# Retention chunks feeding a tanh-shrink MLP: one 64x64 excursion per chunk, single pairs of banks, earlier weight conversions

## The chip, the cores and the metric

The kernel runs on one core of a Trainium2 chip. The metric is device time in microseconds (us) of one execution. Profiled executions give a span, from the first to the last instruction, which is about 2 us shorter than the device time of the same execution.

## The reference

```python
# q, k, v: (4, 8, 768, 64); w_in: (512, 2048); w_out: (2048, 512)
gamma = 1.0 - 2.0 ** (-5.0 - np.arange(H, dtype=np.float32))
for t in range(S):                                   # retention, one state per batch and head
    state = gamma[None, :, None, None] * state + einsum('bhd,bhe->bhde', k[:, :, t], v[:, :, t])
    y[:, :, t] = einsum('bhd,bhde->bhe', q[:, :, t], state) / np.sqrt(D)
x = y.transpose(0, 2, 1, 3).reshape(B * S, H * D)    # 3072 tokens x 512
h = x @ w_in
out = (h - np.tanh(h)) @ w_out
```

The recurrence is computed in chunks of 128 tokens, 24 chunks in all. A **chunk** goes through four stages on TensorE: *turn* (8 transposes of k and q), *products* (k by v and k by q, 64 small matmuls), *outputs* (y from the state and half of the part inside the chunk) and *outputs_rest* (the other half). A **step** of the MLP is one tile: *up_step* (h, 16 matmuls), *shrink_step* (h - tanh h by ScalarE and VectorE, ends in g) and *downs* (o, 8 matmuls, two steps later). There are 96 steps. Weights arrive as 8-byte numbers and are *converted* by ScalarE, then VectorE, then GpSimd (POOL).

## The kernel before

All PSUM tiles of a chunk come from one function with two pairs of banks in rotation. Transposes, products and y of any chunk take the pair that is free next (only the transposes of chunks 0 to 3 use banks of o and h instead).

```python
def banks(name):
    return ps.tile([P, 2, BANK], F32, tag="t", name=name)      # the pool has bufs=2
```

The stages of a chunk, cut to the tiles and the copies that read them:

```python
def turn(ci, tag="t"):
    turned[ci] = [banks(f"kqTp_{ci}")]                # PSUM
    ...                                               # 8 transposes, whole array
def turn_copy(ci):
    nc.scalar.copy(out=t[:, ds(at, n)], in_=tp...)    # kqT, ScalarE, PSUM to SBUF
def products(ci):
    sp = banks(f"s_{ci}")
    ...                                               # 32 + 32 matmuls on 64x64 quarters
    nc.vector.tensor_tensor(m, halves[:, :, 0], ...)  # the mask
    ...                                               # two additions: states
def outputs(ci):
    yT = banks(f"y_{ci}")
    ...                                               # 32 of state, 16 of intra, on quarters
    def rest():
        intra(False)                                  # 16 more on quarters
        nc.scalar.copy(out=xT[n]..., in_=y)           # xT, ScalarE
```

The start is written out by hand, statement by statement. The loop over steps then places a chunk beside chosen steps:

```python
when = [4, 5, 6] + list(range(7, 28, 2)) + [28, 29, 30, 31]
with_chunk = {s: 6 + i for i, s in enumerate(when)}
for s in range(BEGUN, len(steps)):
    ci = with_chunk.get(s)
    if ci is not None:
        scale_chunk(ci + 2)
        outputs(ci)                    # first excursion to quarters
    ...
    up_step(s)
    if ci is not None:
        outputs_rest(ci)               # second excursion
        products(ci + 1)
        load_chunk(ci + 3)
    shrink_step(s)
    downs(LAG)
    if ci is not None:
        turn(ci + 2)
        turn_copy(ci + 2)
```

## Time and profile before

| | before |
|---|---|
| device time, median of 3 executions | 788.15 us (786.81 to 788.59) |
| span of the profiled execution | 786.7 us |
| end of the transposes of chunk 7, the last statement of the start | 82.25 us |
| rest, from there to the end | 704.45 us |
| TensorE idle in the start / in the rest | 22.9 us / 4.9 us |

The columns are the stretch, its length, the busy time and number of instructions of each engine, the granted clock, and the transfers:

```profile
0.00:82.25 82.25, 59.36 (x960) 43.21 (x960) 50.80 (x85) 35.50 (x68) 28.92 (x28) 0.83 0.72 165
82.25:786.70 704.45, 699.55 (x4545) 468.64 (x4544) 471.36 (x724) 334.75 (x593) 94.81 (x79) 1.00 0.16 42
```

Length minus busy time of TensorE is its idle time: 82.25 - 59.36 = 22.9 and 704.45 - 699.55 = 4.9. The start and the rest are thus two different programs, one bound by waits and one by TensorE, and everything below is told for each by itself.

### The profile page before, as it was taken

Reading aid. Unit: us, or ns where it says so; the run is one execution under the profiler, and the core shown is the slowest. Engines: PE = TensorE matmul, PEld = TensorE weight load, DVE = VectorE, ACT = ScalarE, POOL = GpSimd, SP = SyncE. Lnnn points to the kernel's source line nnn. Section 1 sums busy time; section 2 is a strip of 40 time slices with the busy share of each in tenths; the row PEclk is TensorE's granted clock in tenths of the full one; section 3 lists DMA queues with packets and bytes.
Section 4 is the critical chain, followed back from the end, with each engine's and each line's share of the span. In section 5 each row is a group of like instructions: output and inputs, shape, how many; then the busy total and the mean of one; then the engine's idle time right before and its main releaser. Section 6 shows DMA issues by size and latency. Waiting matters only on the chain.

```text
span 786.7 us, 13754 instructions
## 1 busy us (share of the span) xinstructions
PE 758.9 (96%) x5504; PEld 511.9 (65%) x5504; DVE 522.2 (66%) x808; ACT 370.2 (47%) x661; POOL 123.7 (16%) x106
## 2 busy tenths in 40 slices
PE   4869999999999999999999999999999999999997
PEld 4645776677667667666666666666666666666664
DVE  4676698789888875575666565566565656655654
ACT  3453566665655654443344444344444433444432
POOL 1155354333544441000000000000000000000000
PEclk9778999999999999999999999999999999999999
DMA  9953364443433422010000000000000000000000
GB/s 203 260 123 68 87 159 118 123 110 95 120 97 95 105 45 68 29 54 1 1 27 1 0 27 1 1 27 0 13 14 1 27 1 0 27 0 1 28 0 27
DMA packets 85711, 42.97 MB, mean 55 GB/s; under 512 B 76304, under 2 KB 76432, under 8 KB 85648
## 3 DMA queue, kind: packets, MB, share of 16 engines
q1 hardware_dynamic: 85504, 41.95, 21.2%
q8 instruction: 43, 0.70, 0.4%
q10 hardware_dynamic: 144, 0.15, 0.1%
q14 instruction: 20, 0.16, 0.1%
HBM read 35.80 MB, written 6.29 MB: 54 GB/s over the span
## 4 chain that ended last, share of the span: by engine, by line
PE 92%; DVE 4%; SPq 1%; issue 1%; ACT 1%; POOL 1%; DMA 1%; DVEq 0%; POOLq 0%; ACTq 0%
PE o L385 42%; PE h L353 42%; PE y L297 3%; PE kqTp L223 2%; PE s L257 1%; PE s L251 1%; SPq L199 1%; DVE head L176 1%; DVE head L174 1%; DMA raw<-in_moe_w_in_dram 1%; DVE a L261 0%; DVE power L178 0%; POOL low L179 0%; POOL w L183 0%; DVE head L172 0%
## 5 line engine op out<-in xcount | busy, mean ns | idle before, releaser
L385 PE MATMUL o<-w,g 128*128 128x512 f32 x768 | 351.8, 601 | 5.8 <-POOL w L183 5.3
L353 PE MATMUL h<-xT,w 128*128 128x256 f32 x1536 | 354.1, 384 | 3.0 <-POOL w L183 2.2
L353 PEld LDWEIGHTS h<-xT,w 128*128 128x128 f32 x1536 | 292.4, 192 | 71.8 <-issue 31.3
L385 PEld LDWEIGHTS o<-w,g 128*128 128x128 f32 x768 | 145.4, 192 | 152.6 <-issue 138.2
L362 ACT ACTIVATE u<-h 128x512 f32<-128x512 f32 x96 | 57.4, 598 | 268.6 <-PE h L353 268.6
L367 DVE TENSOR_TENSOR th<-h,th 128x512 f32<-128x512 f32 x96 | 66.2, 690 | 159.2 <-ACT th L363 159.2
L377 DVE COPY_PREDICATED g<-large,th 128x512 f32<-128x512 int32 x96 | 73.8, 769 | 10.6 <-DVE g L376 0.9
L370 DVE SCALAR_TENSOR_TENSOR h<-q,h 128x512 f32<-128x512 f32 x96 | 66.9, 697 | 10.4 <-DVE h L368 0.5
L372 DVE SCALAR_TENSOR_TENSOR h<-q,h 128x512 f32<-128x512 f32 x96 | 66.8, 696 | 10.0
L364 ACT ACTIVATE q<-u,tab 128x512 f32<-128x512 f32 x96 | 69.5, 724 | 0.0
L365 ACT ACTIVATE q<-u,tab 128x512 f32<-128x512 f32 x96 | 69.0, 719 | 0.0
L366 ACT ACTIVATE large<-u,tab 128x512 f32<-128x512 f32 x96 | 68.8, 716 | 0.0
L376 DVE TENSOR_TENSOR g<-h,u 128x512 f32<-128x512 f32 x96 | 66.3, 691 | 3.3
L368 DVE SCALAR_TENSOR_TENSOR h<-u,h 128x512 f32<-128x512 f32 x96 | 65.8, 685 | 0.0
L179 POOL TENSOR_TENSOR low<-low,power 128x512 f32<-128x512 f32 x31 | 39.6, 1277 | 157.4 <-DVE power L178 153.7
L363 ACT ACTIVATE th<-h 128x512 f32<-128x512 f32 x96 | 57.1, 594 | 0.0
L233 ACT COPY kqT<-kqTp 128x1024 f32<-128x1024 f32 (+1 forms) x28 | 24.8, 891 | 53.2 <-PE kqTp L223 53.0
L261 DVE TENSOR_TENSOR a<-s,tab 128x512 f32<-128x512 f32 x24 | 16.6, 690 | 41.5 <-PE s L257 41.4
L183 POOL TENSOR_TENSOR w<-low,head 128x512 f32<-128x512 f32 x31 | 39.8, 1283 | 2.4
L331 ACT COPY xT<-y 128x512 f32<-128x512 f32 x24 | 14.1, 587 | 53.5 <-PE y L297 53.5
L208 POOL TENSOR_TENSOR q<-q,tab 128x512 f32<-128x512 f32 x20 | 22.3, 1115 | 14.9 <-DMA q<-in_q_dram 14.9
L297 PEld LDWEIGHTS y<-kqT,state 64*64 64x64 f32 x704 | 12.9, 134 | 17.9 <-issue 11.7
(37 smaller groups left out, 372.2 us busy)
## 6 DMA issues: line engine op xcount, KB each, us to landing
k<-in_k_dram SPq DMA_DIRECT2D x24, 256.0 KB, 4.6
q<-in_q_dram SPq DMA_DIRECT2D x24, 256.0 KB, 5.1
v<-in_v_dram SPq DMA_DIRECT2D x24, 256.0 KB, 5.4
raw<-in_moe_w_out_dram SPq DMA_DIRECT2D x12, 512.0 KB, 3.7
out_dram<-sum SPq DMA_DIRECT2D x24, 256.0 KB, 2.0
raw<-in_moe_w_in_dram SPq DMA_DIRECT2D x14, 256.0 KB, 3.0
raw<-in_moe_w_in_dram SPq DMA_DIRECT2D x28, 128.0 KB, 4.2
raws<-in_moe_w_out_dram SPq DMA_DIRECT2D x4, 512.0 KB, 5.4
```

The source lines that it names most:

```text
L353: nc.tensor.matmul(hp[:, ts(i, TH)], w1[:, c, ts(2 * m2 + i, P)], xT[n // 2][:, c, ts(n % 2, TH)], start=(i == 0 and c == 0), stop=(c == N ...
L362: nc.scalar.activation(u, hp, AF.Square)
L364: nc.scalar.activation(q0, u, AF.Square, bias=bias0)
L365: nc.scalar.activation(q1, u, AF.Square, bias=bias1, scale=math.sqrt(A))
L366: nc.scalar.activation(large, u, AF.Relu, bias=bias_m)
L367: nc.vector.tensor_tensor(th, hp, th, op=ALU.subtract)
L368: nc.vector.scalar_tensor_tensor(hp, in0=u, scalar=R, in1=hp, op0=ALU.subtract, op1=ALU.mult, reverse0=True)
L370: nc.vector.scalar_tensor_tensor(hp, in0=q0, scalar=C0, in1=hp, op0=ALU.add, op1=ALU.mult)
L372: nc.vector.scalar_tensor_tensor(hp, in0=q1, scalar=A * C1, in1=hp, op0=ALU.add, op1=ALU.mult)
L376: nc.vector.tensor_tensor(flat, hp, u, op=ALU.mult)
L377: nc.vector.copy_predicated(flat, large.bitcast(I32), th)
L385: nc.tensor.matmul(o_p[j], gT[n, m2][:, i, ts(j, P)], w2[:, 2 * m2 + i], start=(first and i == 0), stop=(last and i == 1))
```

## The change

The intent has three parts. **One excursion**: the quarter work of three chunks (rest of one, products of the second next, outputs of the next) is put together between downs and the next up_step, so that TensorE leaves whole-array work once for each chunk instead of twice. **Banks**: as this work overlaps two chunks' y, y of even and odd chunks share one fixed pair, and transposes and products share the other, each with one buffer. **Conversions first**: in the start, the weight conversions stand ahead of the masks and shrinks in the queues of VectorE and POOL.

```diff
-    def banks(name):
-        return ps.tile([P, 2, BANK], F32, tag="t", name=name)
+    def banks(tag, name):
+        return ps.tile([P, 2, BANK], F32, tag=tag, name=name, bufs=1)
... (k and q get two buffers instead of three, v four)
-            turned[ci] = [banks(f"kqTp_{ci}")]
+            turned[ci] = [banks("t", f"kqTp_{ci}")]
...
-        sp = banks(f"s_{ci}")
+        sp = banks("t", f"s_{ci}")
...
+    y_banks = banks("y", "y").rearrange("p r (two n t) -> p two r n t", two=2, n=2)
...
-        yT = banks(f"y_{ci}")
-        y = yT[:, :, : 2 * P].rearrange("p r (n t) -> p r n t", n=2)
+        y = y_banks[:, ci % 2]
... (the "seen" copies: four small ones instead of two)
... (the start; here from chunk 2 on, cut)
+    convert(2)
     products(2)
...
-    convert(2)
+    convert(3)
     outputs(2)
     products(3)
...
-    convert(3)
+    convert(4)
     outputs(3)
+    convert(5)
     outputs_rest(3)
...
+    up_step(1)
     shrink_step(0)
-    up_step(1)
-    convert(4)
-    shrink_step(1)
     scale_chunk(4)
-    convert(5)
     up_step(2)
     turn(4)
     turn_copy(4)
-    shrink_step(2)
+    shrink_step(1)
+    convert(6)
     downs(LAG)
     products(4)
     scale_chunk(5)
-    convert(6)
     turn(5)
     turn_copy(5)
     convert(7)
-    up_step(3)
+    shrink_step(2)
     outputs(4)
     products(5)
... (the loop)
-    when = [4, 5, 6] + list(range(7, 28, 2)) + [28, 29, 30, 31]
-    with_chunk = {s: 6 + i for i, s in enumerate(when)}
+    when = [4, 5, 6] + list(range(7, 28, 2)) + [28, 29, 30, 31, 32]
+    with_chunk = {s: 5 + i for i, s in enumerate(when)}
...
-            scale_chunk(ci + 2)
-            outputs(ci)
+            scale_chunk(ci + 3)
+            outputs_rest(ci)
+            products(ci + 2)
+            load_chunk(ci + 4)
+            if ci + 1 < NCH:
+                outputs(ci + 1)
         up_step(s)
-        if ci is not None:
-            outputs_rest(ci)
-            products(ci + 1)
-            load_chunk(ci + 3)
         shrink_step(s)
         downs(LAG)
         if ci is not None:
-            turn(ci + 2)
-            turn_copy(ci + 2)
+            turn(ci + 3)
+            turn_copy(ci + 3)
```

More of the change, by code (lines that the diff above doesn't have):

```diff
@@ L197, in load_chunk @@
         for nm, src in (("k", k), ("q", q), ("v", v)):
-            t = inp.tile([P, H, D], F32, tag=nm, name=f"{nm}_{ci}")
+            t = inp.tile([P, H, D], F32, tag=nm, name=f"{nm}_{ci}", bufs=4 if nm == "v" else 2)
             nc.sync.dma_start(out=t, in_=src[b, :, ts(j, P), :].rearrange("h p d -> p h d"))
@@ L281, in outputs @@
         j = ci % CPB
-        n, nj = divmod(ci, BLK)
-        if nj == 0:
-            xT[n] = xp.tile([P, NP, BLK * P], F32, tag="xT", name=f"xT_{n}")
-        vh = loaded.pop(ci)[2]
+        vh = loaded[ci][2]
         qT = turned.pop(ci)[:, 1]
         a_, st = masked.pop(ci), states.pop(ci)
-        yT = banks(f"y_{ci}")
-        y = yT[:, :, : 2 * P].rearrange("p r (n t) -> p r n t", n=2)
+        y = y_banks[:, ci % 2]
         begun = set()
@@ L318, in outputs @@
         intra(True)
-        flat = yT.rearrange("p r w -> p (r w)")
         for col in range(2):
-            r = ds(D * col, D)
-            s0, s1 = 2 * P - 1 - D, BANK + 2 * P - 1
-            if col:
-                s0, s1 = 2 * P - 1, BANK + 2 * P - 1 - D
-            nc.scalar.copy(out=seen[r], in_=flat[r, s0 : s1 + 1 : s1 - s0])
+            for r in range(2):
+                nc.scalar.copy(out=seen[ds(D * col, D), r : r + 1],
+                               in_=y[ds(D * col, D), r, 1, ds(D * ((r + col) % 2), 1)])
         def rest():
+            n, nj = divmod(ci, BLK)
+            if nj == 0:
+                xT[n] = xp.tile([P, NP, BLK * P], F32, tag="xT", name=f"xT_{n}")
             intra(False)
+            loaded.pop(ci)
             nc.scalar.copy(
@@ L437 @@
     load_weights(1)
-    load_chunk(2)
     scale_chunk(0, nc.vector)
@@ L443 @@
     products(0)
+    load_chunk(2)
     turn(1, "h")
@@ L455 @@
     outputs_rest(1)
-    load_chunk(4)
-    load_weights(6)
-    load_weights(7)
     up_step(0)
@@ L463 @@
     scale_chunk(3, nc.vector)
+    convert(2)
     products(2)
+    load_chunk(4)
+    load_weights(6)
+    load_weights(7)
     turn(3, "o")
     turn_copy(3)
-    convert(2)
+    convert(3)
     outputs(2)
     products(3)
+    load_chunk(5)
     outputs_rest(2)
-    load_chunk(5)
-    convert(3)
+    load_weights(8)
+    convert(4)
     outputs(3)
+    convert(5)
     outputs_rest(3)
-    load_weights(8)
-    load_chunk(6)
+    up_step(1)
     shrink_step(0)
-    up_step(1)
-    convert(4)
-    shrink_step(1)
     scale_chunk(4)
-    convert(5)
     up_step(2)
@@ L485 @@
     turn_copy(4)
-    shrink_step(2)
+    shrink_step(1)
+    convert(6)
+    load_weights(9)
     downs(LAG)
     products(4)
+    load_chunk(6)
     scale_chunk(5)
-    convert(6)
-    load_weights(9)
     turn(5)
@@ L495 @@
     load_weights(10)
-    up_step(3)
+    shrink_step(2)
     outputs(4)
     products(5)
-    outputs_rest(4)
     load_chunk(7)
-    shrink_step(3)
-    outputs(5)
+    up_step(3)
     scale_chunk(6)
-    downs(LAG)
-    outputs_rest(5)
-    load_chunk(8)
     turn(6)
     turn_copy(6)
+    outputs_rest(4)
     products(6)
+    load_chunk(8)
+    outputs(5)
+    shrink_step(3)
+    downs(LAG)
     scale_chunk(7)
```

## The prediction

> **What bounds the kernel now.** I read the page's busy times first, then its slices, then the chain that ended last in order of time, then the timelines of the engines where the chain leaves TensorE.
>
> ```profile
> PE 758.9 (96%) x5504; PEld 511.9 (65%) x5504; DVE 522.2 (66%) x808; ACT 370.2 (47%) x661; POOL 123.7 (16%) x106
> ...
> PE   4869999999999999999999999999999999999997
> PEclk9778999999999999999999999999999999999999
> ```
>
> TensorE is busy 96% of 786.7 us. From the fifth slice (about 80 us) it never idles, so there only less TensorE time can help. The 28 us of idle time and the reduced clock lie before 84 us: a second regime, bound by waits. The chain of the steady part, one chunk in two steps (start us, duration us, what; each piece runs from the end of the one before):
>
> ```profile
> 227.24 3.46 PE h L353 x16
> 230.70 3.43 PE o L385 x8
> 234.13 0.86 PE y L297 x48
> 234.99 3.65 PE h L353 x16
> 238.64 0.39 PE y L297 x16
> 239.03 0.47 PE s L251 x32
> 239.50 0.47 PE s L257 x32
> 239.97 3.63 PE o L385 x8
> 243.60 0.87 PE kqTp L223 x8
> ```
>
> h after whole-array work takes 3.46, h after quarter work (64x64) 3.65; o likewise 3.43 and 3.63. So leaving quarters costs 0.20. Entering: 16 y take 0.39, 48 take 0.86, so 32 more cost 0.47 and 16 without entry would be 0.23; the entry is 0.16. One excursion costs 0.36 beyond its work. Check on the cycle: it lasts 244.47 - 227.24 = 17.23; two plain steps are 2 x 6.89 = 13.77; remainder 3.46. Of that, 128 quarter instructions are 4 x 0.465 = 1.86, transposes 0.87, leaving 0.73 for two excursions. They agree.
>
> In the start, the chain leaves TensorE for the conversion of weights:
>
> ```profile
> 37.03 0.70 DVE head L176
> ...
> 38.39 1.28 POOL low L179
> 39.75 1.28 POOL w L183
> 41.07 5.08 PE h L353 x12
> ...
> 53.93 1.28 POOL low L179
> ...
> 55.29 1.27 POOL w L183
> 56.61 5.49 PE o L385 x6
> ```
>
> h of step 1 waits 2.2 us and the first o 5.3 us for POOL's last operation of a conversion, which waits for four DVE operations that queued behind a mask or behind the shrinks of two steps.
>
> **What the Trainium skill says.** TensorEngine Tiling (Array Packing), Key Properties: changing the tiling mode, not just the tile, drains TensorE. The trace agrees and prices it: 0.16 in, 0.20 out. PSUM — Partial Sum Buffer, section on bank collisions: TensorE may not write a bank and quadrant while ScalarE reads it, even at other columns; the built changed program obeys, as the first y of a chunk waits for the xT copy of the chunk before, now in the same banks. The trace of before has no such pair in one bank, so it does not test that. TensorE: Matmul & The Clock Gate, Part 1: after an idle window the clock is half, for windows of about 3.4 us. The trace agrees: the granted clock is 0.50 between 36 and 44 us and between 56 and 60 us, after waits.
>
> **The change part by part.**
>
> *Excursions.* Before, a chunk in the loop has two: y (state and first half of intra), then, after h, the other half of intra, s. From the code: 18 chunks x 2 = 36 in the loop, 8 before it, 44. After: the loop has 19 excursions (chunks 5 to 23; one holds the rest of a chunk, the products of the second next, the first outputs of the next), 7 before it, 26. Saved in the loop: 17 x 0.36 = 6.2 us, all on the path, as TensorE is the path. The number of quarter instructions stays.
>
> *Single buffer "t".* The two pairs of banks in rotation become one pair "t" (transposes, then s) and one pair "y". So the products of a chunk wait until ScalarE has copied the transposes that lie in t. Every other step has a chunk from step 7 to 27; there a whole step (6.9 us) lies between transposes and products and the wait is hidden. But with chunks in consecutive steps (4, 5, 6, 7 and 28, 29, 30) transposes stand right before the excursion. The ScalarE timeline gives the price:
>
> ```profile
> 295.32 0.60 PE L223 MATMUL kqTp<-tab,q 128*128 128x128 f32 x4
> 295.96 1.01 ACT L233 COPY kqT<-kqTp 128x1024 f32<-128x1024 f32 x1 [2.01 <-PE kqTp L223]
> ```
>
> Transposes end at 295.92 (e). The copy ends at e + 1.05, products may start at e + 1.09. Without a wait they would start after 16 y: those start at e - 0.07 and take 0.28 to the next group's start, so e + 0.21. Stall 0.88, seven times: 6.2 us. This gives back the whole saving of the loop.
>
> *y of two chunks in one pair.* First y of the next chunk waits for the xT copy. Before, that copy starts 0.53 after the rest of y starts (290.02 and 290.55) and takes 0.59, so it is done at +1.12, +1.16 with the semaphore; y is due after 16 y and 64 s at 0.28 + 0.46 + 0.47 = +1.21. Hidden by 0.05, if ScalarE is idle at that moment; in the timeline it waits for TensorE there. In consecutive steps the copy follows the kqT copy and has the 0.93 of the products to hide behind. I allow 0.5 us in all.
>
> *seen copies.* Four of 0.16 instead of two: +0.33 us each. In the loop off the path (the copies run under h). In the start on the path twice: +0.7 before the first h.
>
> *Loads.* k and q have two buffers, so the load of chunk c+2 waits for the products of c. In the loop 7 us or more stay for 5 us of landing and 1 us of scaling: free.
>
> *Conversions first.* Start, by hand from the durations in the timelines. Up to the second transposes +0.35 to +0.7. Conversion 2 on DVE at 29.7 to 31.8 (2.1 as before), mask and states of chunk 2 to 33.2, conversion 3 (3.0, as before where POOL runs beside it) to 36.0, mask 3 to 37.4, POOL's part of 3 to 38.6. So h of step 1 starts at about 38.8 instead of stopping until 41.07, and two h at the reduced clock end at 48.4 (before: 49.4). The first o no longer waits: conversion 5 leaves POOL at 45.2, g of step 0 is there at 46.6; o at 49.3 instead of 56.6. That is the gain at its largest, 7 us. Then it is lost: DVE has the second shrink (ScalarE starts it only after the kqT copy, at 50.4), conversion 6 and mask 4 in order, to 59.4, and the transposes of chunk 5 need the bank that mask 4 reads (before, there was a second buffer). They end at 62.2, h of step 3 starts at 64.4, before at 64.3, though y 4 and the products 5 are then already done (1.7 us that before came after). Transposes 6 wait the same way for mask 5 behind conversion 7 and the third shrink, to 71.5. I get the end of transposes 7 at 79.5 to 81.5; before, at 82.25.
>
> **Sum.** To the end of transposes 7: 80.3 instead of 82.25, -2.0. From there: -6.2 (excursions) + 6.2 (stalls) + 0.2 (16 y of chunk 5 that before came earlier) - 0.5 (a DVE wait of 0.67 at 82.3 that falls away) + 0.5 = 0.2. Total about -1.8 to -2.5; from 788.15 I say 785.8 us.
>
> **The rivals.** (a) The stalls on the kqT copy do not show, because ScalarE or something else gets there earlier: then -6 more, 780. Against it: the copy cannot start before the transposes end, and 1.01 us is measured. For it only that 0.28 of y could stretch. (b) The start gains in full, 7 us to the loop, because transposes 5 and 6 wait less than I think (the clock stays up, DVE is quicker): 781. For it: the first o really has its 5.3 us wait removed. Against it: DVE's order puts whole shrinks ahead of masks 4 and 5. (c) The single buffers make the start worse: transposes 5 and 6 wait longer, idle time holds the clock at half: 792. (d) The xT wait is exposed in all 19 excursions by 0.3: 791. The margin is only 0.05 us, so this is possible. (e) The 64-row work becomes cheaper in one run, and there are no stalls: saving over 2% would need 16 us; excursions are 44 x 0.36 = 16 us in all, so it cannot.
>
> **Range and chances.** Loop: between -6 and +4; start: between -6 and +4; both ends together are unlikely. 785.8 us, 8 in 10 within 779 to 791. Faster by over 2% (under 772.4): 0.03. Slower by over 2% (over 803.9): 0.02. Within: 0.95.
>
> **What would show it.** In the chain of after, steps with a chunk between 100 and 280 us: one cycle of about 16.87 us instead of 17.23, o following h at 3.43, and no second quarter group. In 280 to 320 us: a wait of s (the line of v,k) for ACT kqT of about 0.9 us, three times, and four times around 78 to 115 us; cycles there of 10.85 instead of 10.34. The first o no longer waits for POOL; instead transposes of chunk 5 and 6 wait for DVE state for 3 us or more each. If y waits for ACT xT in every cycle, (d) is right; if s never waits for kqT, (a) is, and I am wrong by 6 us.

## More of the kernel before

For the comparison later, three rows from TensorE's timeline of the kernel before. The columns are start, duration, engine, line, operation, count, and in brackets the idle time ahead of it with its releaser, where there is any:

```profile
56.61 5.49 PE L385 MATMUL o<-w,g 128*128 128x512 f32 x6 [5.29 <-POOL w L183]
...
63.37 0.66 PE L223 MATMUL kqTp<-tab,k 128*128 128x128 f32 x4
...
64.30 3.62 PE L353 MATMUL h<-xT,w 128*128 128x256 f32 x16
```

After o the transposes of chunk 5 (at 63.37) and h of step 3 (at 64.30) follow without any idle time: whatever they need has long been done, and they have a free pair of banks.

## The result and the profile after

| | before | after | predicted |
|---|---|---|---|
| device time, median of 6 executions each | 787.69 us (785.83 to 788.59) | 794.73 us (793.41 to 796.02) | 785.8 (779 to 791) |
| ratio to before, 95% interval | | 1.0091 (1.0074 to 1.0108) | 0.997 |
| span of the profiled execution | 786.7 | 793.9 | |
| end of the transposes of chunk 7 | 82.25 | 87.90 | 80.3 |
| rest | 704.45 | 706.0 | 704.65 |

A ratio is the mean time of one kernel's fast runs over that of the other's of the same rounds, so it is not quite the ratio of the medians. The profiled execution of the kernel after was the slowest of its six (796.02 us), 1.3 us above their median, so its spans are a little long. The change is within 2%, as predicted, but it is 0.9% slower where 0.3% faster was predicted, and the time lies outside the range. Where I set two changed kernels side by side, I subtract their ratios to before and multiply by 787 us. The runs come from several chips, each with its own executions of the kernel before; by the intervals of the two ratios such a difference is uncertain by about 2 us.

The page of the kernel after, the lines that answer to those of the kernel before:

```profile
PE 753.3 (95%) x5504; PEld 514.5 (65%) x5504; DVE 520.7 (66%) x808; ACT 374.6 (47%) x709; POOL 121.1 (15%) x106
...
PE   4765999999999999999999999999999999999997
...
PEclk9887999999999999999999999999999999999999
```

TensorE has 5.6 us less to do (753.3 instead of 758.9), which is the intent of the change. The span is 7.2 us longer all the same, so the idle time grew by 12.8. The busy times by stretch of the kernel after, with the same columns as before, say where:

```profile
0.00:87.90 87.90, 57.78 (x948) 44.89 (x951) 50.81 (x85) 35.68 (x79) 29.28 (x28) 0.84 0.66 149
87.90:793.90 706.00, 695.49 (x4560) 469.65 (x4560) 469.93 (x724) 338.94 (x630) 91.83 (x78) 1.00 0.16 42
```

Start: busy 1.6 less, idle 30.1 instead of 22.9, together +5.65 us. Rest: busy 4.1 less, idle 10.5 instead of 4.9, together +1.55. The start was to become 2 us shorter; that is the larger miss.

**The rest, ordinary chunks.** The chain that ended last, kernel after, one chunk in two steps (start, duration, what):

```profile
249.59 3.46 PE h L352 x16
253.04 3.43 PE o L384 x8
...
258.50 3.65 PE h L352 x16
262.16 3.43 PE o L384 x8
265.59 0.87 PE kqTp L223 x8
266.46 3.46 PE h L352 x16
```

From h to h the cycle lasts 266.46 - 249.59 = 16.87 us instead of 17.23. One h and no o carries the 0.2 of coming back from quarters; before it was one of each. The chain has no ScalarE piece in it: the copies of kqT and xT are hidden here.

**The rest, chunks in consecutive steps.** The same view, where transposes stand right before the excursion. I call this a *direct follow*:

```profile
310.11 0.89 PE kqTp L223 x8
...
311.02 1.02 ACT kqT L233
312.04 0.14 issue
312.18 0.69 PE s L251 x32
```

The chain leaves TensorE for the copy of kqT (1.02 us), passes 0.14 of signalling, and the first products take 0.69 instead of 0.47. From h to h this cycle lasts 11.01 us (303.03 to 314.04 in this chain), while before it was 10.34. Seven such cycles exist. One more bare copy (a copy that no TensorE work covers) stands at step 31, in the same chain:

```profile
332.14 0.44 PE y L295 x16
...
332.60 0.59 ACT xT L330
...
333.24 0.93 PE y L295 x48
```

There are no products left at this place (chunk 24 does not exist), so nothing covers the copy of xT: from 332.14 + 0.44 to 333.24 TensorE stands for 0.66 us, and the following y take 0.93 instead of 0.70: 0.89 us in all.

**The start.** TensorE's timeline of the kernel after (columns as before):

```profile
48.25 6.00 PE L352 MATMUL h<-xT,w 128*128 128x256 f32 x16 [6.01 <-DVE g L375]
...
54.52 0.60 PE L223 MATMUL kqTp<-tab,q 128*128 128x128 f32 x4
54.96 3.60 PE L384 MATMUL o<-w,g 128*128 128x512 f32 x8
...
65.16 1.09 PE L223 MATMUL kqTp<-tab,k 128*128 128x128 f32 x4 [5.51 <-issue]
67.47 1.12 PE L223 MATMUL kqTp<-tab,q 128*128 128x128 f32 x4 [1.22 <-POOL q L208]
...
77.74 0.63 PE L223 MATMUL kqTp<-tab,k 128*128 128x128 f32 x4 [1.49 <-issue]
```

h of step 2 waits 6.01 us for g of step 0. The first o runs at 54.96 without the POOL wait of before. (Before, two of its eight matmuls ran at 50.30 and the other six at 56.61, after the wait.) The products of chunk 4, which follow o, start at 58.48 instead of 62.03, so at this point the kernel is 3.55 us ahead. Then the lead is lost: the transposes of chunk 5 wait 5.51 and 1.22 us, those of chunk 6 1.49, and those of chunk 5 run at half clock (1.09 and 1.12 instead of 0.60; the granted clock is 0.50 from 64 to 72 us). At the end of the transposes of chunk 7 the kernel is 5.65 us behind. So 9.2 us are lost between the first o and that point.

Why do the transposes of chunk 5 wait? VectorE's timeline, kernel after:

```profile
41.99 1.65 DVE L176 SCALAR_TENSOR_TENSOR head<-raws,head 128x512 uint32<-128x512 uint32 x1
...
47.41 0.69 DVE L375 TENSOR_TENSOR g<-h,u 128x512 f32<-128x512 f32 x1
...
57.19 0.69 DVE L366 TENSOR_TENSOR th<-h,th 128x512 f32<-128x512 f32 x1 [8.26 <-ACT th L362]
```

and ScalarE's and POOL's:

```profile
55.16 1.01 ACT L233 COPY kqT<-kqTp 128x1024 f32<-128x1024 f32 x1 [11.77 <-PE kqTp L223]
```

```profile
66.37 1.04 POOL L208 TENSOR_TENSOR q<-q,tab 128x512 f32<-128x512 f32 x1
```

ScalarE stands idle for 11.77 us, because the next thing in its queue is the copy of chunk 4's transposes, and these come after h of step 2. VectorE stands idle for 8.26 us because shrink 1 comes behind that copy on ScalarE. Conversion 6 and the mask and states of chunk 4 stand behind shrink 1 on VectorE, POOL's scaling of q of chunk 5 stands behind POOL's part of conversion 6, and the transposes of chunk 5 need both: the sums for the states of chunk 4, which VectorE still reads out of pair t until 65.05, and the scaled q. (For the transposes of k at 65.16 the profile names only "issue"; that they wait for pair t is read from the code and from these two times.) It is a loop through three in-order queues. The Trainium skill, TensorE: Matmul & The Clock Gate, "Architectural detail: the array is 16× 32×32, not 1× 128×128" in Part 1, states that ScalarE and VectorE are strict first in, first out; this trace agrees, as shrink 1, whose h was done at 42.24 (38.52 and 3.72 long), began on ScalarE only after the copy, at 56.06.

### The profile page after: what moved, and what is told of

It is laid out like the page before. It is cut to its first block, busy times and chain, and to the rows that moved or that the text cites. A ratio compares the mean times of both kernels' runs of the same rounds, so it can differ in the third digit from the quotient of the medians.

```text
span 793.9 us, 13818 instructions
## 1 busy us (share of the span) xinstructions
PE 753.3 (95%) x5504; PEld 514.5 (65%) x5504; DVE 520.7 (66%) x808; ACT 374.6 (47%) x709; POOL 121.1 (15%) x106
## 4 chain that ended last, share of the span: by engine, by line
PE 91%; DVE 4%; ACT 2%; issue 1%; SPq 1%; DMA 1%; POOL 0%; DVEq 0%; ACTq 0%; POOLq 0%
PE h L352 43%; PE o L384 41%; PE y L295 3%; PE kqTp L223 2%; PE s L251 1%; PE s L257 1%; ACT kqT L233 1%; SPq L199 1%; DVE head L174 1%; DVE head L176 1%; DMA raw<-in_moe_w_in_dram 1%; DVE power L178 0%; DVE head L172 0%; DVE h L369 0%; DVE h L371 0%
## 5 line engine op out<-in xcount | busy, mean ns | idle before, releaser
L384 PE MATMUL o<-w,g 128*128 128x512 f32 x768 | 345.6, 593 | 0.5 <-DVE g L376 0.5
L376 DVE COPY_PREDICATED g<-large,th 128x512 f32<-128x512 int32 x96 | 76.2, 793 | 9.8
L223 PE MATMUL kqTp<-tab,k 128*128 128x128 f32 x96 | 16.0, 293 | 11.7 <-issue 7.0
L223 PEld LDWEIGHTS kqTp<-tab,k 128*128 128x128 f32 x96 | 12.5, 150 | 21.5 <-issue 21.1
L295 PEld LDWEIGHTS y<-a,v 64*64 64x64 f32 x768 | 16.8, 140 | 12.6 <-ACT large L365 7.6
L321 ACT COPY seen<-y 64x1 f32<-64x1 f32 x96 | 10.1, 154 | 30.4 <-PE y L295 30.1
```

The source lines that it names most:

```text
L376: nc.vector.copy_predicated(flat, large.bitcast(I32), th)
L384: nc.tensor.matmul(o_p[j], gT[n, m2][:, i, ts(j, P)], w2[:, 2 * m2 + i], start=(first and i == 0), stop=(last and i == 1))
```

## The experiments

Twelve kernels were run, all with correct results. They were meant to tell apart three theories of why the start is late. **A**: because of the wait of h of step 2, which the prediction missed. **B**: because of the banks that were given up, as transposes in a single pair t wait for the products before them. **C**: because of the loop of queues just told, entered through shrink 1 behind the copy of chunk 4's transposes. For the rest of the program the theory is that seven direct follows and the bare xT eat the saving of the 17 excursions.

### a1. Shrink 0 ahead of conversions 4 and 5 (after, one move)

```diff
     load_weights(8)
-    convert(4)
     outputs(3)
-    convert(5)
     outputs_rest(3)
     up_step(1)
     shrink_step(0)
+    convert(4)
+    convert(5)
     scale_chunk(4)
```

> The changed kernel with the shrink of step 0 put ahead of conversions 4 and 5. Theory A (the start lost its time because the up matmuls of step 2 wait for the g that frees their PSUM bank, and g stood behind the two conversions on VectorE): the 6.0 us wait of h for DVE g falls under 1.5 us, the transposes of chunk 5 start 5 to 7 us earlier than 67.5, the time falls by 4 to 7 us, to 788 to 791. Rival B (the single pair of banks t and the transposes' wait for the mask set the start whatever comes before): the wait moves to the transposes of chunk 5 and the time falls by less than 2 us.

Measured: 797.09 us, ratio 1.0114 (1.0099 to 1.0129). TensorE's timeline of this kernel:

```profile
44.47 3.69 PE L352 MATMUL h<-xT,w 128*128 128x256 f32 x16 [1.79 <-DVE g L375]
...
54.92 1.11 PE L223 MATMUL kqTp<-tab,q 128*128 128x128 f32 x4 [6.33 <-POOL q L208]
```

The wait of h is cut from 6.01 to 1.79 us, as meant, and nothing is gained: the transposes of q of chunk 4 now wait 6.33 us for POOL, whose scaling stands behind the two conversions. They start at 54.92, against 54.52 in the kernel after. A falls as a sole cause. The wait was one of two ways through the same queue.

### a2. The loop's chunks in every other step only (after)

```diff
-    when = [4, 5, 6] + list(range(7, 28, 2)) + [28, 29, 30, 31, 32]
+    when = [4, 5, 6] + list(range(8, 40, 2))
```

> The changed kernel with the chunks of the loop in steps 4, 5, 6 and then every other step from 8 to 38, so that only three excursions, not seven, follow their own transposes directly. Theory A (each direct follow costs a wait for the ScalarE copy of the transposes, measured at 11.01 us for such a cycle, which is 1.04 more than 10.34 less the 0.36 saved): waits of s for ACT kqT fall from 8 to 4 and the time falls by 4 x 1.04 = 4.2 us, to about 790.5. Rival B (the waits hide something else that then shows, as deadlines of weights or loads): fewer waits, but less than 2 us gained. The start stays as it is, transposes 7 end near 87.9.

Measured: 791.31 us, ratio 1.0042 (1.0016 to 1.0068), so 0.49% or 3.9 us less than after. The waits of products for kqT are 4 instead of 8. Four direct follows are gone (steps 7, 28, 29 and 30; the bare xT at the end stays); at the 11.01 - 10.34 + 0.36 = 1.03 us of the chain that is 4.1. So the direct follows cost, within the 2 us of uncertainty, what the chain shows.

### a3. Both together

> Both edits. If they are independent (one in the start, one in the loop) the gains add: 794.7 - 4.2 - 4 to 7, so 783.5 to 786.5, just below the kernel before (787.7). If the start's gain is swallowed later, 788 to 790.

The edit is the two above. Measured: 792.54 us, ratio 1.0055 (1.0036 to 1.0073). The first branch of the expectation missed by six us or more, because it counted on the wait of h as A does; the second (788 to 790) by 2.5. The result is near what a1 and a2 give by themselves.

### b1. The early conversions alone, in the kernel before

```diff
     scale_chunk(3, nc.vector)
+    convert(2)
     products(2)
...
-    convert(2)
+    convert(3)
     outputs(2)
...
-    convert(3)
+    convert(4)
     outputs(3)
+    convert(5)
     outputs_rest(3)
...
     up_step(1)
-    convert(4)
     shrink_step(1)
     scale_chunk(4)
-    convert(5)
```

> The kernel before, with its double buffer t, its loop and its excursions, and only the conversions 2 to 5 moved ahead of the masks and the first shrinks. Theory A (the order of conversions is itself what costs): h of step 2 waits for DVE g for 3 to 6 us, the first o no longer waits for POOL, the kernel is 0 to 3 us slower than before. Rival B (the order is good, only the single buffer spoils it): no long wait of h for g, 3 to 6 us faster than before.

Measured: 785.82 us, ratio 0.9974 (0.9959 to 0.9989): 2 us faster than before. The gain is a little less than B allowed for, and B's "no long wait of h for g" was wrong; but A, which forecast that wait and expected a loss of up to 3 from it, has the wrong sign. This is the decisive run on A. TensorE's timeline of this kernel:

```profile
48.02 6.47 PE L353 MATMUL h<-xT,w 128*128 128x256 f32 x16 [5.71 <-ACT q L365]
...
55.20 3.60 PE L385 MATMUL o<-w,g 128*128 128x512 f32 x8
...
59.82 0.66 PE L223 MATMUL kqTp<-tab,k 128*128 128x128 f32 x4
```

In it h of step 2 waits 5.7 us, much as in the kernel after (the profile names a ScalarE operation that ended at 47.90; g of step 0, which frees the bank, ended at 47.87), and the first o runs at 55.20, no earlier than in the kernel after (54.96). But then nothing waits in front of the transposes of chunk 5: they start at 59.82 instead of 65.16, and the transposes of chunk 7 end at 80.45 instead of 87.90. The rest lasts 704.45, to the hundredth that of before. So the earlier conversions are good for 2 us, even with that wait, and what makes the start of the kernel after late lies behind the first o.

### c1. Shrink 1 ahead of the copy of chunk 4's transposes (after, one statement)

```diff
     up_step(2)
+    shrink_step(1)
     turn(4)
     turn_copy(4)
-    shrink_step(1)
     convert(6)
```

> The changed kernel with one statement moved: the shrink of step 1 ahead of the transposes of chunk 4 and their ScalarE copy. Theory C (new, since putting the shrink of step 0 first only moved the loss: the start is set by a loop through the queues, in which the shrink of step 1 stands on ScalarE behind the copy of transposes 4, conversion 6 on VectorE behind that shrink, the scaling of q 5 on GpSimd behind conversion 6, and transposes 5 wait for all of it): the 8.3 us hole of VectorE before that shrink closes, transposes 5 start 4 to 6 us earlier (now k at 65.2, q at 67.5), about 4 to 5 us of the time go: 789 to 791. Rival A (the wait of h of step 2 for g is what counts): that wait stays at 6.0 here, so the time should stay near 794. Rival B (the single pair t): transposes 5 keep waiting 4 us or more for the states of chunk 4.

Measured: 791.07 us, ratio 1.0052 (1.0031 to 1.0074), so 3.1 us less than after. VectorE's timeline of this kernel:

```profile
48.32 0.67 DVE L366 TENSOR_TENSOR th<-h,th 128x512 f32<-128x512 f32 x1
```

The hole of 8.26 us ahead of shrink 1 is closed (it begins at 48.32 instead of 57.19), and the transposes of chunk 5 start at 60.94 and 62.37 instead of 65.16 and 67.47. The wait of h of step 2 is still 6.0. C is right in kind, with 3.1 us where 4 to 5 were expected, and A once more not needed. The profiled execution shows 6.1 us less, but it was the fastest of four of this kernel (789.8 to 792.3), and that of the kernel after was its slowest of six; I go by the timed 3.1. The transposes of chunk 5 still wait 1.65 and 0.80, those of chunk 6 2.21.

### c2. Masks ahead of the next conversion as well

Built on the one before:

```diff
     turn_copy(5)
+    outputs(4)
+    products(5)
+    load_chunk(7)
     convert(7)
     load_weights(10)
     shrink_step(2)
-    outputs(4)
-    products(5)
-    load_chunk(7)
```

> c1 and the outputs of chunk 4 and products of chunk 5 put ahead of conversion 7 and the shrink of step 2, so that the mask of chunk 5, which frees the single pair t for transposes 6, no longer stands behind them on VectorE. If the single pair has a cost in the start beside theory C, the 1.5 us wait of transposes 6 goes and the time falls by 1 to 2 us more than c1: about 788. If not: as c1 within 0.7 us.

Measured: 792.1 us, ratio 1.0065 (1.0041 to 1.0089), no gain over c1. The wait ahead of the transposes of chunk 6 is now for POOL's q (2.89 us), which stands behind conversion 7. The wait only changed its name.

### e1. Conversion 6 behind chunk 4's products (on c1)

```diff
-    convert(6)
     load_weights(9)
     downs(LAG)
     products(4)
     load_chunk(6)
     scale_chunk(5)
+    convert(6)
```

> c1 (the changed kernel with the shrink of step 1 ahead of transposes 4) with conversion 6 moved behind the mask of chunk 4 and the scaling of q 5. If conversion 6 ahead of them is the rest of what the order costs: the 0.8 us wait of transposes 5 for q goes, 1 to 2 us below c1 (791.07), 789 to 790. If the rest belongs to the single pair: transposes 5 still wait 1.6 us for the states of chunk 4, and the time stays within 0.7 us of c1.

Measured: 791.6 us, ratio 1.006 (1.0048 to 1.0073): no gain over c1. The wait for POOL's q is gone, but the transposes of chunk 5 still wait 1.65 us for the states of chunk 4, and those of chunk 6 now 4.62. The second branch of the expectation holds: the time stays within 0.7 us of c1. In both waits the transposes start about 0.1 us after VectorE has read the last states out of pair t.

### c3 and c4. The reorderings and the spread together

> c2 with the chunks of the loop spread to every other step, which took 3.9 us off the changed kernel. The start and the loop are separate, so the gains add: c2 less 3.5 to 4 us, about 784, and clearly below the kernel before.

The edit is c2's with a2's. Measured: 787.73 us, ratio 1.0007 (0.9985 to 1.0028), 4.6 us less than c2. The spread is worth in this start what it was in the other, but the sum stayed 4 us above the expectation, as c2's start had not gained.

> c3 with the shrink of step 0 ahead of conversions 4 and 5, and the scaling of q and v 4 ahead of them on GpSimd. By theory C the shrink of step 0 first did not help because transposes 4 then waited 6.3 us for q 4 behind conversions 4 and 5 on GpSimd. With q 4 ahead that wait goes and h of step 2 waits under 2 us: 1 to 4 us below c3, 780 to 783. If the first o then waits for conversion 5 as long as h did for g, no gain over c3.

This is c3 with the scaling of chunk 4 and shrink 0 ahead of conversions 4 and 5. Measured: 786.63 us, ratio 0.9997 (0.9979 to 1.0015). The wait of h is gone and the first o waits 3.8 us for POOL instead. So none of the orders built on the kernel after brings it below the kernel before by more than the interval.

### d2. Transposes covered by downs (after, the loop only)

```diff
         up_step(s)
-        shrink_step(s)
-        downs(LAG)
         if ci is not None:
             turn(ci + 3)
+        shrink_step(s)
+        if ci is not None:
             turn_copy(ci + 3)
+        downs(LAG)
```

> The changed kernel with the loop's transposes put between the up matmuls and the down matmuls of their step, and their ScalarE copy behind the shrink's ScalarE work, so that 3.4 us of down matmuls lie over the copy. Theory (each of the six direct follows inside the loop costs 1.04 us of waiting for the copy, and the seventh, before the loop, stays): waits of s for ACT kqT fall from 8 to 2, the time falls by 6 x 1.04 = 6.2 us, to about 788.5. Rival: the transposes, now 3.4 us earlier, wait for the mask that frees t or for the scaled q, and less than 3 us is gained. The start is unchanged.

Now o (3.4 us) lies between the transposes and the products. Measured: 789.26 us, ratio 1.0029 (1.001 to 1.0048), 4.9 us less than after. Of the 8 waits for kqT, 2 are left, both beside the start. The busy times of this kernel after the end of its start (columns as before):

```profile
85.77:785.70 699.93, 694.22 (x4561) 468.84 (x4560) 469.68 (x725) 337.75 (x630) 94.08 (x80) 1.00 0.16 43
```

The rest lasts 699.9 us instead of 706.0, so 6.1 less, against 6 x 1.03 = 6.2. This settles the loop: the merged excursions are worth the saving once no direct follow eats it. (The start of this execution was 2.1 us shorter than that of the profiled execution of after, with the same statements up to the loop. Starts of one program differ by so much.)

### d3. The start of b1 with the merged loop of d2

```diff
-    def banks(name):
-        return ps.tile([P, 2, BANK], F32, tag="t", name=name)
+    pairs = [ps.tile([P, 2, BANK], F32, tag=x, name=x, bufs=1) for x in ("t", "y")]
+    turn_of = [0]
+    in_loop = [False]
+    def banks(name):
+        if in_loop[0]:
+            return pairs[0]
+        turn_of[0] += 1
+        return pairs[turn_of[0] % 2]
... (outputs as in the change once in_loop; the loop as in d2)
+    in_loop[0] = True
     for s in range(BEGUN, len(steps)):
```

> The start of the kernel before, with the conversions ahead of the masks and two pairs of banks in rotation (the order that ran at 785.8 us), and then the loop of the changed kernel with one excursion for each chunk, single t, y of two chunks in one pair, and the transposes before the down matmuls. If start and loop are separate: transposes 7 end near 80.5, the loop from there 704.4 - 6.2 (17 excursions) + 0.9 (the xT copy laid bare where no products follow) + up to 1 at the seam, about 700; the time is 780.5 to 783, 0.6 to 0.9 percent below the kernel before, and better than both kernels. If the seam costs more, or transposes wait for masks, 784 to 787.

Measured: 780.68 us (780.41 to 781.58), ratio 0.9917 (0.9899 to 0.9934). It is faster than both kernels: 6.5 us under before, 13.7 under after. The transposes of chunk 7 end at 79.96, and the rest lasts 699.6. (The buffers of k, q and v and the four "seen" copies are those of the kernel after, so these are not what costs.)

### e3. The same with the single pairs in the start

```diff
-    in_loop = [False]
+    in_loop = [True]
```

> The hybrid that ran at 780.7 us, with one thing changed: the start too has the single pair t for transposes and s, and one pair for y, as the changed kernel has; the order of statements stays. It measures the single pair's own cost in the start. If it has one (transposes 5 wait for the states of chunk 4, whose mask stands behind the shrink of step 2 on VectorE and ended at 62.9, instead of starting at 59.3, and transposes 7 for the states of chunk 6): 3 to 5 us slower than the hybrid, 784 to 786. If only the order of statements cost: 780.5 to 782.

Measured: 785.49 us, ratio 0.9985 (0.9971 to 0.9999), so 0.68% or 5.4 us slower than d3 (the two ran on different chips, each against before on its own). One word differs; it makes t a single pair in the start and puts every y there into the other one. TensorE's timeline of this kernel:

```profile
60.91 1.12 PE L229 MATMUL t<-tab,k 128*128 128x128 f32 x4 [3.41 <-DVE state L280]
...
82.00 1.14 PE L257 MATMUL t<-v,k 64*64 64x64 f32 x32 [1.19 <-ACT kqT L239]
```

Transposes of chunk 5 wait 3.41 us for the states of chunk 4, which VectorE still has to add out of pair t, and those of chunk 7 wait 1.67. Products wait twice 1.19 us for kqT. In d3 all that is left of this kind is one wait for kqT of 0.48 and one for states of 0.74. B is right, with a size. TensorE's waits of y for xT are the same in both (4 waits, 2.9 us in all), so what shows is pair t and not the shared pair of y. d3 in turn waits longer for the states that y reads (6.0 us in all instead of 2.9), so the cost is less than the sum of e3's new waits.

e3 can also be set against d2: both have the single pairs and the same loop, and only the order of the start's statements differs (the loads among them, and the rest of chunk 5, which e3 has in the start and d2 in the loop). e3 is 0.44% or 3.5 us faster. Then each step from the kernel before to the kernel after has its own pair of timed runs: earlier conversions -2.0 (b1 against before), merged excursions without direct follows -4.5 (d3 against b1), single pairs in the start +5.4 (e3 against d3), the new order of the start's other statements +3.5 (d2 against e3), direct follows +4.9 (after against d2). The five add up to the measured +7.2 by construction; what they show is the share of each, to about 2 us.

## Why the prediction was wrong

**Excursions, right.** The cycle of an ordinary chunk is 16.87 us, as predicted to the hundredth. The price of 0.36 for one excursion stood up.

**Stall on the single buffer t in the loop, right in kind and number, 0.15 too small each.** Predicted 0.88, seven times. The cycle in consecutive steps is 11.01 instead of 10.34 us, so it costs 0.67 net of the 0.36 saved, or 1.03 (the expectations say 1.04). The term that was mis-sized is the stall, "products may start at e + 1.09" less "e + 0.21". Products start 1.18 after the transposes' end in the chain (0.02, 1.02 and 0.14). Without a wait they would start 0.39 after it, which is what 16 y take in an ordinary chunk's chain. So the wait itself is 0.79, even a little less than predicted. What the term left out is that after a wait the first 32 products take 0.69, not 0.47. That is 0.79 + 0.22 = 1.01. a2 and d2 agree with the size (3.9 us for four, 6.1 for six).

**xT hidden, right with one exception.** In ordinary and in consecutive chunks xT is never on the chain, so rival (d) did not happen. The prediction reasoned from a full excursion; at step 31 there are no products to hide the copy, and 0.89 us (0.66 idle and 0.23 slower y) are missing in its sum.

**The rest as a sum.** -17 x 0.36 + 7 x 1.03 + 0.89 + 0.2 - 0.5 = 1.7 (the last two terms are the prediction's); measured 1.55, predicted 0.2. (17 x 0.36 is 6.1, not the 6.2 of the prediction.) "This gives back the whole saving of the loop" was right, and a little more than that.

**The start, wrong.** Predicted 80.3, measured 87.90 in the profiled execution: 7.6 us, where the median time was missed by 8.9. The "seen" copies were no part of this: each group grew from 0.33 to 0.45 us, not by 0.33. h of step 1 came at 38.52, predicted 38.8. The first step that failed is "two h at the reduced clock end at 48.4". It had g of step 0 done at 46.6 (measured 47.41 to 48.10) but overlooked that h of step 2 takes the bank of step 0's h, which shrink 0 works in until that g. So h of step 2 started at 48.25, ended at a granted clock of 0.59 at 54.25, and all that I had set on it came 5.7 us later: o at 54.96 instead of 49.3. Set against the prediction's own times, 5.7 of the 7.6 us enter here, 0.6 more by the end of the transposes of chunk 5 (68.5 instead of 62.2), 1.0 by h of step 3 (71.71 instead of 64.4) and 0.3 after it. g itself is late partly because VectorE shares its way to memory with POOL. The operation at 41.99 took 1.65 us beside POOL's at 41.75, where it takes 0.69 alone. The Trainium skill, SBUF — State Buffer, section on the two sides, states that the pair of ports which VectorE and GpSimd share is locked for a whole instruction and the loser blocks; the trace agrees, as it ended 0.56 after POOL's did.

But this step is not what makes the kernel slower than before. The same wait is in b1, which is faster than before, and a1 takes it away without gain, as POOL's scaling of q then waits behind the same conversions: the o at 49.3 that the prediction counted on was out of reach by both ways. What makes it slower stands in good part in the prediction as rival (c), at 792: "The single buffers make the start worse"; the other part, the order of the statements (shrink 1 behind the copy), it had only in its main line (transposes of chunk 5 wait for mask 4, behind the second shrink and conversion 6), with the end of the transposes of chunk 5 at 62.2; it was 68.5, since the missed wait came ahead of the same queue. So of the 7 us gained at the first o, which were to be lost partly, only 3.55 were there, and the loss of 9.2 us outweighed them.

One reading of the trace in the prediction is loose: the half clock from 36 to 44 us in the kernel before sets in after waits of only 0.27 to 0.68 us, so this stretch does not show the idle window that the prediction names; the one from 56 to 60, after 5.29 us of idle time, does.

**What is shown, and its size.** The earlier conversions gain 2 us (b1). The single pair in the start costs about 5.4 us (e3 against d3). The new order of the start costs about 3.5 us (d2 against e3), and shrink 1 behind the copy, which is part of it, about 3 us (c1). In the loop, six of the direct follows cost 6.1 us by the profiles and 4.9 by the timed rounds (d2), and without them merging gains 704.45 - 699.9 = 4.6 us.

**What stays open.** The sizes for the start don't add up to its +5.65 exactly: -2 + 5.4 + 3.5 is 6.9. Each is uncertain by about 2 us, and part of e3's cost lies beyond the start's end: its rest lasts 702.89 us against 699.64 in d3, with a granted clock of 0.63 between 82 and 90 us where d3 has 1.00 between 80 and 87. The start also varies from one execution to the next by about 2 us, so single profiled spans say less about it than the timed rounds do. The traces show where: the reduced clock falls on different work. After and d2 have the same start, but from 77 to 85 us the granted clock is 0.79 in after and 1.00 in d2; and h of steps 1 and 2 take 3.72 and 6.00 us in after, 5.41 and 5.38 in d2, 5.91 and 3.69 in c2. A slow h of step 1 costs little, as h of step 2 waits for g in any case: in c2 the first o starts at 53.26 instead of 54.96. Why the clock falls so or so was not tried.

## What to carry to other kernels

Merging excursions to another tiling mode pays a fixed price each (0.36 us here), so count them. Then count the buffers given up for the merge: a tile with one buffer needs other TensorE work between its write and the next use, and here moving the transposes ahead of o was all that was missing in the loop. Where a start is bound by waits, follow every new wait through the in-order queues to the bank it holds, and keep the second buffer there even if the steady part no longer needs it.

## What the Trainium skill lacked or had wrong

- TensorEngine Tiling (Array Packing), Key Properties, says that changing the mode drains TensorE but not what it costs: 0.16 us in and 0.20 out between 128x128 and 64x64 fp32 work, and a cycle of 16.87 instead of 17.23 us with one excursion less.
- None of the pages cited here has the price of handing a PSUM copy back to TensorE when it is bare: for kqT 1.02 us of copy, 0.14 of signalling, and 0.22 more for the first 32 products; 1.03 us per cycle in all, net of the 0.39 us of y that would run meanwhile.
- SBUF — State Buffer states that the loser of the shared ports blocks; how much of a start this can take isn't told: in this trace VectorE operations of 0.43 and 0.69 us took 1.38 and 1.65 us beside POOL's.
